# Attention and two feed-forward blocks on one core: the rows of maxima are written into q's stack by DMAs of GpSimd's queue in place of SyncE's

## The chip, the cores and the metric

The kernel runs on one core of a Trainium2 chip. The metric is the device time of one execution, in microseconds (us); less is better. Of several runs the median counts. The engines are named as in the profile: PE is TensorE (PEld its weight loads), DVE is VectorE, ACT is ScalarE, POOL is GpSimd, SP is SyncE. SPq marks SP's DMA-issuing instructions.

## The reference

```python
def _attn_ref(q, k, v, g_q, g_k):              # q, k, v: 4 x 12 x 448 x 64
    q_n, k_n = (rmsnorm(q, g_q), rmsnorm(k, g_k))
    scores = 1.0 / np.sqrt(64) * np.matmul(q_n, k_n.transpose(0, 1, 3, 2))
    scores = scores - np.max(scores, axis=-1, keepdims=True)
    attn = np.exp(scores)
    attn = attn / (np.sum(attn, axis=-1, keepdims=True) + 1e-09)
    return np.matmul(attn, v)

def _moe_ref(x, w_in, w_out, g_ln):            # x: 1792 x 768, d_ff 1024
    h = x @ w_in
    solu = h * softmax(h)
    return layer_norm(solu, g_ln) @ w_out

def _moe2_ref(x, w_in, w_out):                 # d_ff 2048
    h = x @ w_in
    return (h - np.tanh(h)) @ w_out
```

The attention output is put into rows of 768 and goes through the first feed-forward block, then the second. Everything is float32.

## The kernel before, in words

float32 products are made of rounded parts: an operand is split into a high part (`hi`) and a rest (`lo`), and `hi*hi + hi*lo + lo*hi` is summed in PSUM.

**Attention.** The 48 heads are taken in 24 pairs `p`, the heads of a pair being `n = 2p` and `n = 2p + 1`. For a pair, q and k are loaded (`load_qk`), normalised (`norm`, whose last products are L266 on POOL), transposed on PE and split (`qk_trans`, giving `wq` and `wk`). Their parts are stacked by DMA into one of three wide buffers each, `Q[p % 3]` (q_157, q_158, q_159 in listings of the built program) and `K[p % 3]` (k_154 to k_156): 128 rows, of which 64 hold one part and 64 another, so that one matmul sums two products.

The softmax needs the maximum of each row of scores. `maxima` makes the high-part scores on PE (`mps`, L350 and L342), and DVE takes their negated maximum (`nm`, L351). `spread` then turns four columns of `nm` into four rows by a transpose on PE (`nmps`, L358), ACT copies these to SBUF (`nt`, L360; 4 partitions x 128), and a DMA of 2 KB lays them as one row of 512 into q's stack (L363). In the stack of k the matching row is ones, so that the second matmul of each score tile adds the negated maximum to the scores. The scores proper are `weights` (`sps`, L386; L380 to L383 for the first pair): for every block of 128 keys two matmuls, of which the first needs the high stack only and **the second needs the row of maxima**. ACT takes the exponential (`pf`, L395), and `pv` multiplies it with v (`pvps`, L409). So for each of the 48 heads there is this line: DVE's maxima, PE's transpose, ACT's copy, the DMA of L363, PE's second `sps` matmul.

**The order.** The parts of attention stand in a list `attn` with a slot and a step each (`at`, `step`): the maxima of head n at steps 4n to 4n+3, `spread` at 4n+4, its weights from 4n+7 (`LAG`). The first feed-forward block (`moe_h`, `moe_x2`, `moe_lnT`, `layer_norm`) is laid over the attention of the next batch by `overlap`, which interleaves the two by costs. Over this a scheduler of the framework orders the instructions of each engine by a simulated timeline, so the final order differs from that of the code.

**The queues.** SP issues nearly all DMAs, in its order: the loads of q, k and v, the stacks (L309, L313, L315, L316), the weights as raw 64-bit words (L115), their converted copies written out and read again (L164, L178, L182), x and x2 (L440, L504, L624), and the 48 rows of L363. An instruction that waits holds up those behind it on the same engine. POOL issues no DMA; in the attention part it does L266, the last subtraction of a weight conversion (L161), the fill of v's ones (L230, a memset), the power in `layer_norm` (L591) and a few copies of zeros (L320).

After the attention (from about 515 us on) the rest of the first block and the second block (`h2`, `out2`) run, with PE busy all the time.

Of the kernel before, what the change touches and what calls it, by code (L numbers as in the profile page):

```python
# [8 lines left out]
F32 = mybir.dt.float32  # L9
# [9 lines left out]
def kernel(  # L19
# [14 lines left out]
    nc = tc.nc  # L34
    B, H, S, D = q.shape
# [19 lines left out]
    NQ = 3  # L55
# [146 lines left out]
    Q, K, qd = [], [], []  # L202
# [6 lines left out]
    QW, GAP = 4 * S + 64, 64  # L209
# [143 lines left out]
    def spread(n):  # L353

        p, i = divmod(n, 2)
        o = 64 * i if p == 0 else 64 - 64 * i
        ps = ps_m.tile([128, 128], F32, tag="m", name="nmps")
        nc.tensor.transpose(ps[:4], nm_t[p][:, 3 * i:3 * i + 4], idf)  # L358
        nt = A["small"].tile([4, 128], F32R, tag="nt", name="nt")
        nc.scalar.activation(out=nt, in_=ps[:4], func=AF.Copy)  # L360

        c = ((2 + i) * S + GAP if p == 0 else QO[i, 1]) - GAP * i
        nc.sync.dma_start(out=Q[p % NQ][o:o + 1, c:c + S + GAP].bitcast(F32), in_=nt.bitcast(F32))  # L363

    def weights(n, j):

# [85 lines left out]
    for p in range(NP):  # L452
        s = 2 * p
        at(s - 7, 0, load_qk, p)
        if 1 <= p <= NQ:
            at(s - 2 if p < NQ else 4, 1, fill, p % NQ)
            at(s - 2 if p < NQ else 4, 1, fill_q, p % NQ)
        at(s, 1, load_v, p)
        at(s - 3, 1, norm, p)
        at(s - 2, 2, qk_trans, p, 1)  # L460
        at(s - 1, 0, qk_trans, p, 0)
        for i in range(2):
            n, z = s + i, 4 * (s + i)
            for j, c in enumerate((3, 0, 1, 2) if i == 0 else (4, 5, 6)):
                step(z + j, maxima, p, c)
            step(z + 4, spread, n)
            for j in range(3):
                step(z + LAG + j, weights, n, j)
                step(z + LAG + 4 + j, pv, n, j)
        step(z + LAG + 3, weights, s + 1, 3)  # L470
        step(z + LAG + 4, pv_tails, s)
        step(z + LAG + 4, pv_fin, s)
        step(z + LAG + 6, pv_fin, s + 1)
        step(z + LAG + 8, x_norm, p)
# [237 lines left out]
    for z in range(2):  # L712
        o = slice(64 * z, 64 * z + 64)
# [165 lines left out]
```

## Time and the profile before

| | before |
|---|---|
| runs | 1109.31 us median of 3 (1105.35 to 1111.76) |
| profiled execution: span from the first to the last instruction | 1107.5 us |
| profiled execution: its own time | not recorded apart from the span |
| PE busy / PEld busy | 1043.3 us (94%) / 864.2 us (78%) |
| DVE / ACT / POOL busy | 690.5 / 493.1 / 236.4 us |
| mean granted TensorE clock | 0.983 |
| q's rows of maxima (L363) | 48 DMAs of 2 KB, all of SP |

Busy time of an engine is the time in which its instructions run; the issue of a DMA is not counted in it. In rows of waits, a row says who waited (engine, line, tile), for what, the total in us, the number of times and the longest one. "x2" behind an instruction in a timeline is a run of two, told as one; a bracket behind it is the idle time of the engine just before and what ended it.

### The profile page before, as it was taken

To read this page: it belongs to the slowest core of one execution; us is meant where nothing else is said; L and a number is where in the kernel's file an instruction comes from. 1 tells how busy PE (TensorE), PEld (TensorE's weight loads), DVE (VectorE), ACT (ScalarE), POOL (GpSimd) and SP (SyncE) were. 2 spreads that over 40 slices of the span, in tenths; PEclk is the share of its full clock that TensorE was granted. 3 is DMA by queue.
4 is the path that set the end of the run, shared out by engine and by line. 5 is a ranking of instruction groups with operands and counts; after the bars stand their busy time and mean duration, and the time that the engine had idled before them with its cause. 6 is when DMAs were issued, how large, how long until landed. Compare 5 with 4: busy or idle time off the path is not lost.

```text
span 1107.5 us, 15169 instructions
## 1 busy us (share of the span) xinstructions
PE 1043.3 (94%) x5348; PEld 864.2 (78%) x5348; DVE 690.5 (62%) x1311; ACT 493.1 (45%) x994; POOL 236.4 (21%) x204
## 2 busy tenths in 40 slices
PE   4989999989887899999999999999999999999998
PEld 2555566648664678778889989898999989898988
DVE  8766686787787453633684066475767666675444
ACT  4667776777677455555255154311212121212110
POOL 2511123121102110001420034242414141322000
PEclk9999999989988999999999999999999999999999
DMA  7987789866996987666786443021112111110004
GB/s 182 274 227 192 179 216 281 207 181 178 284 320 185 327 229 216 192 209 203 227 291 208 138 162 95 23 74 39 57 40 59 55 58 58 57 57 1 1 29 171
DMA packets 113743, 171.16 MB, mean 155 GB/s; under 512 B 31940, under 2 KB 79492, under 8 KB 113668
## 3 DMA queue, kind: packets, MB, share of 16 engines
q1 hardware_dynamic: 112368, 170.20, 52.8%
q8 instruction: 42, 0.69, 0.3%
q14 instruction: 33, 0.27, 0.1%
q10 hardware_dynamic: 1300, 0.01, 0.1%
HBM read 109.32 MB, written 29.10 MB: 125 GB/s over the span
## 4 chain that ended last, share of the span: by engine, by line
PE 72%; DMA 15%; DVE 6%; ACT 4%; issue 1%; SPq 1%; POOL 1%; ACTq 0%; DVEq 0%; POOLq 0%
PE pvps L409 9%; PE ops L191 7%; PE ops L192 7%; PE ops L190 7%; PE h2ps L191 7%; PE h2ps L192 7%; PE h2ps L190 7%; PE sps L386 4%; DMA raw<-in_moe_w_out_dram 3%; PE x2ps L190 3%; PE x2ps L191 3%; PE x2ps L192 3%; DMA q<-nt 2%; DMA raw<-in_moe_w_in_dram 2%; DMA w<-w_in 2%; PE mps L350 1%
## 5 line engine op out<-in xcount | busy, mean ns | idle before, releaser
L820 DVE TENSOR_TENSOR ob<-ops,ob 128x384 f32<-128x384 f32 x196 | 108.5, 554 | 104.1 <-PE ops L192 103.6
L161 POOL TENSOR_TENSOR w<-val,w 128x512 fp32r<-128x512 f32 x60 | 82.5, 1377 | 424.6 <-ACT w L160 397.0
L409 PE MATMUL pvps<-pf,va 128*128 128x448 f32 (+1 forms) x384 | 164.9, 598 | 0.9 <-ACT pf L395 0.9
L191 PE MATMUL ops<-w,gT 128*128 128x384 f32 x448 | 150.6, 336 | 0.0
L190 PE MATMUL ops<-w,gT 128*128 128x384 f32 x448 | 150.3, 336 | 0.0
L192 PE MATMUL ops<-w,gT 128*128 128x384 f32 x448 | 150.2, 335 | 0.0
L351 DVE TENSOR_REDUCE nm<-mps 128x1 f32<-128x448 f32 x168 | 102.6, 617 | 71.1 <-PE mps L350 61.2
L192 PE MATMUL h2ps<-x2s,w 128*128 128x512 f32 (+1 forms) x384 | 140.9, 367 | 0.0
L386 PE MATMUL sps<-q,k 128*128 128x448 f32 (+1 forms) x368 | 118.1, 415 | 24.2 <-DMA q<-nt 9.7
L191 PE MATMUL h2ps<-x2s,w 128*128 128x512 f32 (+1 forms) x384 | 140.9, 367 | 0.0
L190 PE MATMUL h2ps<-x2s,w 128*128 128x512 f32 (+1 forms) x384 | 140.5, 366 | 0.0
L797 ACT ACTIVATE th<-h2ps 128x512 f32<-128x512 f32 (+1 forms) x64 | 34.8, 544 | 182.5 <-PE h2ps L192 182.3
L386 PEld LDWEIGHTS sps<-q,k 128*128 128x128 f32 (+1 forms) x368 | 63.0, 186 | 60.2 <-ACT pf L395 17.6
L395 ACT ACTIVATE pf<-sps 128x448 f32<-128x448 f32 x167 | 88.3, 539 | 38.5 <-PE sps L386 32.5
L409 PEld LDWEIGHTS pvps<-pf,va 128*128 128x128 f32 (+1 forms) x384 | 63.4, 202 | 42.9 <-issue 35.6
L190 PE MATMUL hps<-w,xs 128*128 128x256 f32 (+1 forms) x276 | 90.6, 329 | 2.6 <-DMA w<-w_in 2.6
L266 POOL TENSOR_TENSOR qn<-qk,rr 112x512 f32<-112x512 f32 x44 | 49.0, 1135 | 195.8 <-DVE rr L247 74.7
L350 PE MATMUL mps<-k,q 128*128 128x448 f32 (+1 forms) x144 | 78.4, 553 | 11.1 <-ACT pf L395 3.3
L191 PEld LDWEIGHTS ops<-w,gT 128*128 128x128 f32 x448 | 84.2, 188 | 4.7
L190 PEld LDWEIGHTS ops<-w,gT 128*128 128x128 f32 x448 | 84.2, 188 | 4.4
L192 PE MATMUL hps<-w,xs 128*128 128x256 f32 (+1 forms) x276 | 85.9, 313 | 0.0
L191 PE MATMUL hps<-w,xs 128*128 128x256 f32 (+1 forms) x276 | 85.7, 311 | 0.0
(118 smaller groups left out, 2042.0 us busy)
## 6 DMA issues: line engine op xcount, KB each, us to landing
w<-w_out SPq DMA_DIRECT2D x48, 512.0 KB
raw<-in_moe_w_in_dram SPq DMA_DIRECT2D x36, 512.0 KB
raw<-in_moe_w_out_dram SPq DMA_DIRECT2D x36, 512.0 KB
w<-w_in SPq DMA_DIRECT2D x24, 512.0 KB
k<-wk SPq DMA_DIRECT2D x46, 224.0 KB
q<-wq SPq DMA_DIRECT2D x46, 224.0 KB
w_in<-w SPq DMA_DIRECT2D x12, 512.0 KB
w_out<-w SPq DMA_DIRECT2D x12, 512.0 KB
```

The lines of the kernel that those rows point to most:

```text
L161: nc.gpsimd.tensor_tensor(out=w[:, 1], in0=x, in1=w[:, 0].bitcast(F32), op=ALU.subtract)
L190: nc.tensor.matmul(ps, lhsT=a[0], rhs=w[0], start=first, stop=False)
L191: nc.tensor.matmul(ps, lhsT=a[0], rhs=w[1], start=False, stop=False)
L192: nc.tensor.matmul(ps, lhsT=a[1], rhs=w[0], start=False, stop=last)
L266: eng.tensor_tensor(out=qn[:, a].rearrange("p c h d -> p h c d"), in0=t[:, a], in1=rr[:, a].rearrange("p h (c o) -> p h c o", o=1).to_broa ...
L350: nc.tensor.matmul(ps, lhsT=qh[:, f:f + 128], rhs=kh, start=True, stop=True)
L351: nc.vector.tensor_reduce(out=nm_t[p][:, c:c + 1], in_=ps, axis=AX.X, op=ALU.max, negate=True)
L386: nc.tensor.matmul(o, lhsT=K[p % NQ][:, i, z, k0:k0 + m], rhs=qcols(Q[p % NQ], slice(0, 128), p, i, z), start=(z == 0), stop=(z == 1))
L395: nc.scalar.activation(out=x, in_=ps, func=AF.Exp)
L409: nc.tensor.matmul(pv_t[n], lhsT=w, rhs=pc_t.pop((n, j))[r], start=first, stop=last)
L797: nc.scalar.activation(out=th, in_=ps, func=AF.Tanh)
L820: nc.vector.tensor_tensor(out=o, in0=ps, in1=o, op=ALU.add)
```

## The change

One line of `spread`: the DMA is issued on GpSimd's queue instead of SyncE's.

```diff
@@ def spread(n)
         nt = A["small"].tile([4, 128], F32R, tag="nt", name="nt")
         nc.scalar.activation(out=nt, in_=ps[:4], func=AF.Copy)
 
         c = ((2 + i) * S + GAP if p == 0 else QO[i, 1]) - GAP * i
-        nc.sync.dma_start(out=Q[p % NQ][o:o + 1, c:c + S + GAP].bitcast(F32), in_=nt.bitcast(F32))
+        nc.gpsimd.dma_start(out=Q[p % NQ][o:o + 1, c:c + S + GAP].bitcast(F32), in_=nt.bitcast(F32))
```

The order of the built program changes with it, on the queues and, through the scheduler, on other engines.

SP, in the middle of the attention (pair 12; q and k are the stacks, xd the attention's output, va the tile of v), as a difference:

```order
 L236 DMA va<-in_v_dram 128x1x64
 L440 DMA xd<-xo 128x448
-L363 DMA q_157<-nt 1x4x128
 L309 DMA q_158<-wq 64x2x448 x2
 L313 DMA q_158<-wq 64x448 x2
-L363 DMA q_157<-nt 1x4x128
 L316 DMA k_156<-wk 64x448 x2
```

The two rows of the pair leave SP; the stacks of the next pair follow the store of x directly.

POOL, from pair 7 to pair 9 (qn is the normalised q and k, w a converted weight tile), as a difference:

```order
+L363 DMA q_158<-nt 1x4x128
+L363 DMA q_159<-nt 1x4x128
 L161 TENSOR_TENSOR w_1450<-val,w_1450 128x512
 L161 TENSOR_TENSOR w_1726<-val,w_1726 128x512
+L363 DMA q_159<-nt 1x4x128
 L266 TENSOR_TENSOR qn<-qk,rr 112x2x4x64 x2
 L161 TENSOR_TENSOR w_1739<-val,w_1739 128x512
 L230 MEMSET va 128x7x64
+L363 DMA q_157<-nt 1x4x128 x2
 L161 TENSOR_TENSOR w_1752<-val,w_1752 128x512
```

The rows now stand between POOL's own instructions, and those behind them wait for ACT's copy with them.

PE, around the first use of pair 2's rows (the stack q_159), as a difference:

```order
-L386 MATMUL sps<-q_159,k_156 128x448 x2
+L386 MATMUL sps<-q_159,k_156 128x448
+L409 MATMUL pvps<-pf,va 128x448 x3
 L342 MATMUL mps<-wk,qd_151 128x448
 L358 MATMUL nmps<-idf,nm 4x128
+L386 MATMUL sps<-q_159,k_156 128x448
+L409 MATMUL pvps<-pf,va 128x448 x2
 L276 MATMUL qkps<-idf,qn 128x112 x4
-L409 MATMUL pvps<-pf,va 128x448 x3
-L386 MATMUL sps<-q_159,k_156 128x448 x2
-L409 MATMUL pvps<-pf,va 128x448 x3
+L386 MATMUL sps<-q_159,k_156 128x448 x2
```

The second `sps` matmul, the one that needs the row, now has three `pvps` matmuls, the `mps` and the next transpose ahead of it.

## Rows read from the trace of the kernel before

**Rows 1.** The page's chain that ended last, by line, shares of the span.
```profile
PE pvps L409 9%; PE ops L191 7%; PE ops L192 7%; PE ops L190 7%; PE h2ps L191 7%; PE h2ps L192 7%; PE h2ps L190 7%; PE sps L386 4%; DMA raw<-in_moe_w_out_dram 3%; PE x2ps L190 3%; PE x2ps L191 3%; PE x2ps L192 3%; DMA q<-nt 2%; DMA raw<-in_moe_w_in_dram 2%; DMA w<-w_in 2%; PE mps L350 1%
```

**Rows 2.** Windows: length, busy us per engine, PE clock, DMA share, GB/s.
```profile
0.00:500.00 500.00, 441.54 (x2113) 314.76 (x2113) 340.17 (x704) 327.75 (x707) 92.65 (x105) 0.96 0.82 227
500.00:1107.00 607.00, 601.73 (x3237) 549.39 (x3235) 350.34 (x607) 165.31 (x288) 143.73 (x99) 1.00 0.30 95
```

**Rows 3.** Waits of PE from 0 to 510 us.
```profile
PE sps L386 <- DMA q<-nt: 9.7, 7, 2.7
PE sps L386 <- ACT pf L395: 9.0, 11, 1.9
PE sps L386 <- DVE nm L351: 4.7, 4, 2.9
...
PE hps L190 <- DMA w<-w_in: 2.6, 4, 0.9
...
PE sps L383 <- DMA q<-nt: 0.6, 1, 0.6
```

**Rows 4.** Timeline around four of PE's eight stops for a row.
```profile
22.32 0.27 ACT L360 ACTIVATE nt<-nmps 4x128 fp32r<-4x128 f32 x1 [0.41 <-PE nmps L358]
25.07 0.71 PE L383 MATMUL sps<-q,k 64*128 64x448 f32 x1 [0.62 <-DMA q<-nt]
...
55.48 0.27 ACT L360 ACTIVATE nt<-nmps 4x128 fp32r<-4x128 f32 x1 [0.52 <-PE nmps L358]
55.77 0.76 SPq L363 DMA_DIRECT2D q<-nt  x1
62.40 0.47 PE L386 MATMUL sps<-q,k 128*128 128x448 f32 x1 [2.73 <-DMA q<-nt]
...
217.34 0.25 ACT L360 ACTIVATE nt<-nmps 4x128 fp32r<-4x128 f32 x1
219.59 0.66 SPq L363 DMA_DIRECT2D q<-nt  x1
222.61 0.47 PE L386 MATMUL sps<-q,k 128*128 128x448 f32 x1 [1.57 <-DMA q<-nt]
...
239.09 0.25 ACT L360 ACTIVATE nt<-nmps 4x128 fp32r<-4x128 f32 x1
244.15 0.74 PE L386 MATMUL sps<-q,k 128*128 128x448 f32 x1 [1.73 <-DMA q<-nt]
```

**Rows 5.** Timeline: copies and the weight loads that need their rows, calm pairs.
```profile
73.18 0.27 ACT L360 ACTIVATE nt<-nmps 4x128 fp32r<-4x128 f32 x1 [0.52 <-DMA qk<-in_k_dram]
75.94 0.30 PEld L386 LDWEIGHTS sps<-q,k 128*128 128x128 f32 x2 [0.41 <-DVE nm L351]
...
126.51 0.27 ACT L360 ACTIVATE nt<-nmps 4x128 fp32r<-4x128 f32 x1 [0.52 <-PE nmps L358]
129.51 1.10 PEld L386 LDWEIGHTS sps<-q,k 128*128 128x128 f32 x6 [0.36 <-DVE nm L351]
...
353.18 0.25 ACT L360 ACTIVATE nt<-nmps 4x128 fp32r<-4x128 f32 x1
355.04 0.57 PEld L386 LDWEIGHTS sps<-q,k 128*128 128x128 f32 x2 [0.55 <-ACT pf L395]
```

**Rows 6.** Windows of a stop and of two half-clock stretches, columns as before.
```profile
59.40:62.40 3.00, 0.27 (x3) 0.01 (x1) 1.11 (x1) 0.21 (x1) 0.00 (x0) 1.00 0.99 270
...
63.26:66.66 3.40, 3.40 (x11) 1.43 (x8) 2.50 (x6) 2.43 (x7) 0.00 (x0) 0.50 0.61 149
...
387.53:390.93 3.40, 3.40 (x9) 2.05 (x7) 1.25 (x2) 0.54 (x1) 0.00 (x0) 0.50 0.96 308
```

**Rows 7.** SP's own waits, from 0 to 500 us, the first row of L363.
```profile
SPq L363 <- ACT pf L395: 15.5, 8, 3.3
```

**Rows 8.** POOL's lines: min, median, max ns of L161; group of L591.
```profile
L161 POOL TENSOR_TENSOR w<-val,w x60: 1265/1293/2642, 24.3 to 1024.6; 128x512 fp32r<-128x512 f32 x60
...
L591 POOL TENSOR_TENSOR rs<-rs,mhalf 128x1 f32<-128x1 f32 x14 | 9.3, 671 | 76.7 <-DVE rs L590 64.9 <-DVE rs L593 10.1 <-DVE rr L247 1.7
```

## The prediction

> **What bounds the kernel now.** I read the chain of waits first, by line [rows 1]. The reader is to see that PE's lines fill most of it, and that `DMA q<-nt`, the row of maxima on its way into q's stack, holds 2% of the span, some 22 us: small, but the largest entry after PE's lines and the weight loads. The windows say where time can be won at all [rows 2]: from 500 us on PE is busy 601.7 of 607 us, so nothing there is to be had; before it PE stands still 500 - 441.5 = 58.5 us, and a microsecond taken out of that moves all that follows. PE's waits split that idle time [rows 3]: the row of maxima is behind 9.7 us of it at `sps`, and 0.6 us at the first pair, 10.3 us in eight stops. ACT's exponentials (9.0) and DVE's maxima (4.7) come next at the same line.
>
> The timeline shows such a stop whole [rows 4]. ACT's copy ends at 55.75, SP issues at once, and PE, which could have gone on at 62.40 - 2.73 = 59.67, goes at 62.40. So the row took 6.65 us where 3.9 were to be had. I call the first number its delay (end of the copy to PE going) and the second its **room**. The issue is 0.7 us of it, so nearly 6 us are flight, and in that window the DMA engines are busy 0.99 of the time [rows 6]: the 2 KB lie behind megabytes which SP issued before. At 217 us the other part shows: the copy ends at 217.59, SP issues 2.0 us later, because it stands at something before it.
>
> A stop costs twice. After that of 2.73 us the granted clock is 0.50 from 63.26 to 66.66, that is 1.2 instead of 2.4 GHz, with PE busy throughout [rows 6]: 3.4 us at half speed do 1.7 us of work. Five such stretches, the first and the last of which are shown, begin within 3 us of a stop for a row.
>
> **The change, part by part.** *SP loses 48 issues.* Each is about 0.66 us [rows 4], 32 us of SP's time, and with them its waits for ACT at L363, of which the largest row alone is 15.5 us [rows 7]. The stacks and loads behind them go out earlier. I cost that at nothing: PE's waits for a weight load are 2.6 us [rows 3], which bounds the gain, and the DMA engines are at their limit where loads are late. Cover: the loads are issued ahead; were it gone, this 2.6 us would grow first.
>
> *POOL gains 48 issues.* No row shows a DMA of POOL. Its price lies between that of POOL's smallest work of the kind, 0.67 us for one column (L591), and that of a subtraction over 512 columns, 1.3 us (L161) [rows 8]. I take 1.0, near the first, since a DMA of four pieces is little work. For the flight I take what SP's rows need in calm stretches: a copy that ended at 73.45 had landed before the second load of the pair that starts at 75.94, so at most 2.6 us after the copy, of which 0.66 are issue; and in the pair at 353 us at most 2.0 us, of which 1.3 are flight [rows 5]. So copy to landing is 1.0 + 1.3 to 1.0 + 1.9, or 2.3 to 2.9 us; I take **3.0** for all, with a little for crowded stretches. The ends: 2.0 us, if POOL issues as fast as SP, and 6.65, the delay of [rows 4], if the flight stays as long as it is.
>
> The Trainium skill (DMA: Bandwidth & Descriptors, Latency and other measured facts) gives the first byte about 1 us after a DMA of GpSimd and 0.6 after one of SyncE; no run here shows that yet, and an estimate from it would be SP's 2.6 plus 0.4, 3.0 us as well.
>
> *The eight stops.* A delay of 3.0 us ends each stop whose room is 3.0 or more. The rooms in [rows 4], as above: 1.86 at the first pair (22.59 to 25.07 - 0.62), 3.92, 3.45 and 3.08; the other four have more. So seven stops go, 9.7 us, and the first grows from 0.62 to 1.14.
>
> *The calm rows pay.* There the row comes just in time now. Rooms in [rows 5], up to the load that needs the row, each load taking 0.19: 2.6 us at 73, 3.6 at 127 (the last of the six loads), 2.0 at 353. Of the first heads of the five pairs copied between 73 and 127 these are the first and the last, the three others about 3. New stops at 3.0: 0.4 and 1.0 us. Second heads have more room, since a whole head's scores come before theirs.
>
> Idle time: 10.3 goes, 1.1 + 0.4 + 1.0 = 2.5 comes, net -7.8. Clock: five stretches of 1.7 go, 8.5; that the two new stops of about 1 us draw one each is the dear assumption, and I take it: 3.4 comes back, net -5.1. Together -12.9.
>
> *What is late next.* At the lines where PE stopped, ACT's and DVE's work is the other thing it waits for [rows 3], 13.7 us beside 9.7. Where the row comes earlier, some of those stops stay with another name. I count two thirds: **-8.6**.
>
> *POOL's queue.* In the order of before and after, most pairs have both rows together, ahead of L266. In five pairs POOL's own work stands between, which holds the second row only, by a subtraction of 1.3 us or two; second heads have the room. What is queued behind a waiting row is L266, L161 and L591; L266's products go to PE's transposes of a later pair, L161's to a store for later. I cost that at nothing; uncovered, it is 1.3 us for each such pair.
>
> *The schedule.* It moves little. Three `pvps` matmuls more before pair 2's row add room at the longest stop.
>
> The sum against the profiled execution: 1107.5 - 8.6 = 1098.9 of span. The median of the runs is 1.8 above the span of before, so 1100.7; I say **1101**.
>
> **The rivals.** *The flight stays long* (chance 0.10). If POOL's row waits in the same DMA engines behind the same bulk, only SP's queueing is saved: 2.0 us at 217, and at the longest stop nothing. That takes away about half of the stops, -5 + 2.5 of idle, and two of five stretches, -3.4, so about -6, two thirds of it -4: 1105. For it: the DMA share of 0.99. Against: 2 KB need not lie behind another queue's megabytes. The Trainium skill (DMA: Bandwidth & Descriptors, Issuing engines are not separate DMA queues) says that all issuers run on the same 16 engines and that another issuer saves only issue time; by that rule this case would hold.
>
> *The next wait takes over* (0.12). ACT's and DVE's lines stop PE at the same places; with a quarter of the sum left, 1106.
>
> *POOL is slow, and it gets slower* (0.15). It is decided at a delay of about 4.1 us from the copy. At 4.0 the stops are 2.1, 0.1, 0.6 and 0.9 in [rows 4], 1.4, three of 1.0, 0.4 and 2.0 in [rows 5]: 10.5, as much as goes. At 5.0 each of the ten is one more, 20.5 against 10.3, and there are ten stretches of half clock against five: +10.2 + 8.5 = 18.7, two thirds 12.5, so 1122. For it: a subtraction of POOL was stretched from 1.27 to 2.64 us, so something can hold POOL. Against: its median is 1.29 [rows 8], so that is rare. The Trainium skill (SBUF — State Buffer, SBUF: two separate sides) says that a DMA of GpSimd cannot write its descriptors while DVE runs an operation that takes the shared port; by that rule POOL's issue would be long where DVE converts weights, and this case would hold there.
>
> *More than that* (0.08): the whole 12.9 and loads earlier by 2.6 us, 1094.
>
> **How the numbers follow.** The forecast has 0.55, with a range of its own from 1094 to 1106. Half a per cent, about what a measurement of this kernel can tell from no change, is 5.5 us: faster is below 1103.8, slower above 1114.9. The forecast gives 0.46 to faster and 0.09 to the same; the long flight 0.02 and 0.08; the next wait 0.10 to the same and 0.02 to slower; slow POOL 0.13 to slower and 0.02 to the same; the last 0.08 to faster. That is 0.56, 0.29, 0.15. For 8 in 10 the range goes from 1090 to 1114: it takes in the whole sum with a few us for the schedule, no gain, and a delay a little above 4.1.
>
> **What would show it.** Right: POOL's DMA instructions take about 1 us; PE's wait for `DMA q<-nt` falls from 10.3 to some 3 us, and is at the first pair and at calm pairs; the half-clock stretches behind PE's stops for a row are gone; SP has no L363. Wrong: POOL's issue of 2 us or more, or waits of `sps` for the row at every calm pair; or the waits for the row gone and PE idle as long before 500 us, with ACT or DVE named. The prediction fails also if the new order delays L266 or `layer_norm` behind a row that waits.

## The result and the profile after

The changed kernel is slower: 1118.88 us median (1116.77 to 1121.97, 6 runs) against 1107.37 us (1104.63 to 1111.76, 6 runs) of before, a ratio of 1.0104 with a 95% interval from 1.0074 to 1.0134, or 11.5 us. The forecast was 1101 us with a range that ended at 1114. Its profiled execution took 1116.77 us, with a span of 1114.5. In the experiments below one run of e1_first_sp (1124.58 us) and one of s1_sp_order (1131.38 us) were in a slower state; they count in the medians and not in the ratios.

The rows of maxima in the changed kernel, by tile (minimum, median, maximum in ns; then from the start of the issue to the landing in us):

```profile
L363 POOL DMA_DIRECT2D q<-nt x48: 521/556/772, 22.6 to 497.8; - x48
...
DMA to landing us min/median/max: 1.5/3.2/8.5
```

GpSimd issues a row in 0.556 us, less than the 1.0 that I assumed. But it lands after 1.5 us only at best, after 3.2 in the median and 8.5 at worst. The stretch makes a difference: here are the landings from 220 to 265 us, where the DMA engines are busy 0.64 of the time, and from 265 to 330 us, where they are busy 0.97.

```profile
DMA to landing us min/median/max: 1.6/2.6/3.6
...
DMA to landing us min/median/max: 4.8/5.3/8.5
```

The windows that answer to [rows 2]:

```profile
0.00:500.00 500.00, 436.96 (x2083) 312.04 (x2084) 342.05 (x704) 322.80 (x698) 117.72 (x153) 0.96 0.81 225
500.00:1107.00 607.00, 605.25 (x3245) 550.61 (x3244) 348.46 (x603) 169.86 (x296) 144.12 (x99) 1.00 0.29 94
```

Before 500 us TensorE stands still for 500 - 436.96 = 63.0 us, where it was 58.5. That is 4.5 us more. All of the loss is ahead of 500 us, for the last copy of `nt` is 7.60 us later and the whole span 7.0. The mean granted clock there is 0.96 in both, but the two decimals hide a few us: the stretches at 0.50 ahead of 500 us sum to 44.4 us where they were 37.5. At half speed that is (44.4 - 37.5) / 2 = 3.5 us, an estimate, and with the 4.5 us about the whole loss. It comes early; the first 70 us before and after (the clock is the third figure from the end):

```profile
0.00:70.00 70.00, 48.74 (x153) 27.37 (x154) 52.10 (x121) 40.47 (x87) 23.91 (x31) 0.95 0.90 231
...
0.00:70.00 70.00, 47.56 (x128) 26.74 (x128) 52.41 (x112) 35.38 (x77) 23.74 (x34) 0.85 0.78 211
```

TensorE's waits up to 510 us, which answer to [rows 3]:

```profile
PE sps L386 <- ACT pf L395: 8.6, 12, 2.2
PE hps L190 <- DMA w<-w_in: 5.4, 2, 4.2
PE x2ps L190 <- DMA w<-w_out: 4.8, 1, 4.8
PE pvps L409 <- ACT pf L395: 4.7, 6, 2.6
PE sps L383 <- DMA q<-nt: 4.6, 1, 4.6
...
PE sps L386 <- DVE nm L351: 2.8, 6, 0.9
...
PE sps L386 <- DMA q<-nt: 1.7, 4, 0.7
```

The wait that the change was to remove did shrink, from 9.7 to 1.7 us. Four others grew: the first pair's row from 0.6 to 4.6, the weights of the first block's input projection (`hps`) from 2.6 to 5.4, and those of its output projection (`x2ps`), one wait of 4.8 where the same view of before has

```profile
PE x2ps L190 <- DMA w<-w_out: 1.3, 2, 1.0
...
PE pvps L409 <- ACT pf L395: 0.9, 3, 0.4
```

The last of these lines is the fourth: `pvps` waits 4.7 us for ACT's exponentials where it was 0.9.

To see where the time goes I compare when ACT makes the same copy of `nt` in two traces. The shift (after less before) is +11.36 us at the 5th copy (66.83 against 55.48; the shifts are of unrounded times), +6.05 at the 12th, +0.40 at the 27th (239.49 against 239.09), +1.04 at the 31st, +5.39 at the 32nd, +9.08 at the 37th and +7.60 at the last. So there are three stretches: a loss up to 67 us, a gain up to 239 us, and a second loss from 282 us on.

The first loss begins at the first pair. Timeline of the changed kernel (answers to the first stop of [rows 4]):

```profile
21.67 0.27 ACT L360 ACTIVATE nt<-nmps 4x128 fp32r<-4x128 f32 x1 [0.27 <-PE nmps L358]
...
22.57 0.77 POOL L363 DMA_DIRECT2D q<-nt  x1 [15.86 <-ACT nt L360]
...
28.38 0.71 PE L383 MATMUL sps<-q,k 64*128 64x448 f32 x1 [4.58 <-DMA q<-nt]
```

The copy is earlier than before, and TensorE goes 3.3 us later. That stop I had put at 1.14 us. From 35.30 to 38.70 us TensorE is busy only 1.93 us; then the granted clock (the figure ahead of the DMA share) falls from 2.4 to 1.2 GHz and stays there for 20 us:

```profile
38.71:59.19 20.48, 20.45 (x46) 11.33 (x46) 13.78 (x27) 8.33 (x19) 8.34 (x9) 0.50 0.82 240
```

The second loss begins at 292 us:

```profile
292.02 0.58 PE L190 MATMUL hps<-w,xs 128*128 128x256 f32 x1 [4.23 <-DMA w<-w_in]
```

### The profile page after: what moved, and what is told of

Its sections match the earlier page's. It is cut to its first block, busy times and chain, and to the rows that moved or that the text cites. A ratio compares the mean times of both kernels' runs of the same rounds, so it can differ in the third digit from the quotient of the medians.

```text
span 1114.5 us, 15196 instructions
## 1 busy us (share of the span) xinstructions
PE 1046.2 (94%) x5348; PEld 866.4 (78%) x5348; DVE 693.2 (62%) x1311; ACT 492.7 (44%) x994; POOL 261.8 (23%) x252
## 4 chain that ended last, share of the span: by engine, by line
PE 70%; DMA 13%; DVE 8%; ACT 3%; issue 3%; POOL 1%; SPq 1%; DVEq 0%; POOLq 0%; ACTq 0%
PE pvps L409 8%; PE ops L191 7%; PE ops L192 7%; PE ops L190 7%; PE h2ps L191 7%; PE h2ps L192 7%; PE h2ps L190 7%; PE sps L386 4%; PE x2ps L190 3%; PE x2ps L191 3%; PE x2ps L192 3%; DMA xr<-xd 2%; DMA w<-w_in 2%; DVE nm L351 2%; DMA q<-nt 2%
## 5 line engine op out<-in xcount | busy, mean ns | idle before, releaser
L161 POOL TENSOR_TENSOR w<-val,w 128x512 fp32r<-128x512 f32 x60 | 81.4, 1360 | 371.4 <-ACT w L160 363.8
L386 PE MATMUL sps<-q,k 128*128 128x448 f32 (+1 forms) x368 | 118.9, 414 | 13.7 <-ACT pf L395 8.6
L386 PEld LDWEIGHTS sps<-q,k 128*128 128x128 f32 (+1 forms) x368 | 62.7, 185 | 49.4 <-ACT pf L395 16.3
L190 PE MATMUL hps<-w,xs 128*128 128x256 f32 (+1 forms) x276 | 91.1, 331 | 5.5 <-DMA w<-w_in 5.4
L363 POOL DMA_DIRECT2D q<-nt x48 | 26.7, 556 | 259.4 <-ACT nt L360 202.4
L190 PE MATMUL x2ps<-lnT,w 128*128 128x384 f32 (+1 forms) x240 | 80.5, 335 | 6.0 <-DMA w<-w_out 5.7
L192 PE MATMUL hps<-w,xs 128*128 128x256 f32 (+1 forms) x276 | 85.9, 314 | 0.0
L138 POOL TENSOR_SCALAR val<-raw 128x512 f32<-128x512 f32 x48 | 79.7, 1660 | 25.6 <-DMA raw<-in_moe_w_out_dram 10.8
```

What stands on the lines that cost most here:

```text
L138: nc.gpsimd.tensor_scalar(out=fv, in0=fh, scalar1=2.0 ** -15, scalar2=None, op0=ALU.max)
L161: nc.gpsimd.tensor_tensor(out=w[:, 1], in0=x, in1=w[:, 0].bitcast(F32), op=ALU.subtract)
L190: nc.tensor.matmul(ps, lhsT=a[0], rhs=w[0], start=first, stop=False)
L192: nc.tensor.matmul(ps, lhsT=a[1], rhs=w[0], start=False, stop=last)
L363: nc.gpsimd.dma_start(out=Q[p % NQ][o:o + 1, c:c + S + GAP].bitcast(F32), in_=nt.bitcast(F32))
L386: nc.tensor.matmul(o, lhsT=K[p % NQ][:, i, z, k0:k0 + m], rhs=qcols(Q[p % NQ], slice(0, 128), p, i, z), start=(z == 0), stop=(z == 1))
```

## The experiments

Executions of one kernel differ: beside the first four experiments the kernel before ran 31 times, from 1099.07 to 1113.06 us. So sizes below are ratios to runs of before taken beside the kernel, with 95% intervals (they are not quite the quotients of the medians), and single traces are used for the place of a loss and for waits that return in several of them. The median of before was 1106.20, 1108.06, 1106.94, 1109.01 and 1106.71 us in the five groups of experiments; 0.1% is 1.1 us.

| kernel | rows of maxima issued by | order of the rest | median us | ratio |
|---|---|---|---|---|
| changed kernel | POOL | its own ("new") | 1118.88 | 1.0104 (1.0074 to 1.0134) |
| e8_after_again | POOL | new | 1121.05 | 1.0134 (1.0079 to 1.0188) |
| e1_first_sp | SP for pair 0, POOL | its own | 1110.84 | 1.0036 (1.0010 to 1.0062) |
| e2_late_sp | POOL up to pair 12, then SP | its own | 1112.17 | 1.0055 (1.0023 to 1.0087) |
| e3_mid_pool | POOL for pairs 1 to 12, else SP | its own | 1106.19 | 0.9996 (0.9966 to 1.0026) |
| e4_act_queue | ACT | its own | 1111.07 | 1.0048 (1.0013 to 1.0083) |
| e5_warm | POOL, one DMA earlier | new | 1117.28 | 1.0101 (1.0059 to 1.0143) |
| e7_sp_twin | POOL, twins on SP | its own | 1116.73 | 1.0080 (1.0053 to 1.0108) |
| e9_pool_twin | SP, twins on POOL | its own | 1114.14 | 1.0055 (1.0021 to 1.0089) |
| e6_only_first | POOL for pair 0, else SP | its own | 1112.65 | 1.0040 (1.0018 to 1.0063) |
| r1_order_before | POOL | that of before ("old") | 1112.81 | 1.0043 (1.0018 to 1.0068) |
| r2_order_after | SP | new | 1119.47 | 1.0111 (1.0075 to 1.0147) |
| r3_first_sp | SP for pair 0, POOL | old | 1108.14 | 1.0013 (0.9985 to 1.0041) |
| s1_sp_order | SP | new on SP, old elsewhere | 1118.07 | 1.0081 (1.0042 to 1.0121) |
| s2_engine_order | SP | old on SP, new elsewhere | 1148.26 | 1.0349 (1.0314 to 1.0384) |
| s3_act_pinned | ACT | old | 1113.55 | 1.0053 (1.0025 to 1.0082) |
| s4_warm_pinned | POOL, one DMA earlier | old | 1111.31 | 1.0028 (1.0004 to 1.0051) |
| t1_order_late | SP | new from pair 13 on | 1116.03 | 1.0096 (1.0068 to 1.0124) |
| t2_order_early | SP | new up to pair 12 | 1110.42 | 1.0026 (1.0002 to 1.0050) |

### Which pairs lose it

```diff
-        nc.gpsimd.dma_start(out=Q[p % NQ][o:o + 1, ...
+        (nc.sync if p == 0 else nc.gpsimd).dma_start(...        # e1_first_sp
+        (nc.sync if p > 12 else nc.gpsimd).dma_start(...        # e2_late_sp
+        (nc.gpsimd if 0 < p < 13 else nc.sync).dma_start(...    # e3_mid_pool
+        nc.scalar.dma_start(...                                 # e4_act_queue
```

e1_first_sp, expected:

> The first pair's two rows go back to SyncE's queue, the other 46 stay on GpSimd's. Theory START (the first row lands 3.3 us later on GpSimd's queue, SyncE's bulk goes out beside it, and TensorE's rise to full clock and its next rows slip with it: 11.4 us lost by 67 us of the span): the shift at the fifth stop (the copy of nt at 55.48 us before, 66.83 us after) falls to within 2 us of before, and the time to about 1108 us (1105 to 1111). Theory LATE (the loss is made from 285 to 420 us, by the weights' loads in SyncE's new order): the shift of 6.5 us there stays, and the time falls by less than 6 us. Theory ORDER (any other order of SyncE's queue scatters the time, no single row is the cause): 1113 to 1121 us with the early shift still over 5 us.

e2_late_sp, expected:

> The rows of pairs 13 to 23 go back to SyncE's queue; those of pairs 0 to 12 stay on GpSimd's. Theory LATE: the shift made from 285 to 420 us (6.5 us) goes, the wait for the output projection's weights falls from 4.8 us towards 1.3, and the time is about 1112 us (1110 to 1115). Theory START alone: the 11.4 us at 67 us stay and are given back by 265 us as in the changed kernel; what happens later does not depend on the queue, so 1117 to 1121 us. Theory ORDER: no more than 3 us either way.

e3_mid_pool, expected:

> Only the rows of pairs 1 to 12 go by GpSimd's queue; pair 0 and pairs 13 to 23 stay on SyncE's. START and LATE together: neither loss is made and the gain of 10.2 us between 67 and 265 us stays, at least in part (the stops that it removes in that stretch): 1096 to 1103 us, faster than before. If the gain between 67 and 265 us was only the recovery of the time lost at the start (the loads run ahead while TensorE is late, so that later waits are shorter), it is not there without the loss: 1105 to 1110 us. ORDER: 1110 to 1120 us.

e4_act_queue, expected:

> All 48 rows go by ScalarE's queue, behind the copy that makes them, so SyncE is relieved as with GpSimd's queue, but GpSimd's way of issuing is left out. If the loss is that of GpSimd's queue (a first packet 2.9 us after the issue at the first row, landings of 1.5, 3.2 and 8.5 us), the first row lands within 0.5 us of its time before and the time is below 1112 us, unless ScalarE's own issue time (unknown; at 0.5 to 1 us each for 48 of them 24 to 48 us of ScalarE's time, part of it on the chain) takes it back. If the loss is that SyncE's bulk is no longer held behind the rows (START by crowding, or ORDER), it stays: 1115 to 1125 us, with the first row late as in the changed kernel.

With the first pair back on SyncE a loss of 0.36% is left, with the late pairs back one of 0.55%, and with both back none: each half seems to cost about as much as the other. But pairs 1 to 12 by GpSimd's queue also gained nothing (0.9996), though it is in their stretch that the changed kernel gained 10 us of shift. So those 10 us were no gain of the change but a recovery of a TensorE that was late at the start. e6_only_first, further down, has it too, with the rows of pairs 1 to 12 on SyncE: its shift is +10.04 us at the 5th copy and +1.92 at the 27th. The rows on ScalarE's queue lose as well (1.0048) with the first row on time (TensorE goes at 24.58 us). So GpSimd's queue need not be the cause, though ScalarE's own 48 issues may be part of that loss.

### What the queue does, and what is only late once

e5_warm puts one DMA of 2 KB on GpSimd's queue at 6.65 us; nothing waits for it.

```diff
     make_identity(nc, idf)
+    warm = const.tile([1, 512], F32, name="warm")
+    nc.gpsimd.dma_start(out=warm, in_=idf[:4, :])
```

> The changed kernel with one more DMA of 2 KB on GpSimd's queue at the very start, which nothing waits for. Theory FIRST USE (the queue's first DMA is slow because it is the first: issue 0.77 us against a median of 0.556, first packet 2.9 us later): the first row is then an ordinary one and lands some 1.5 us after its issue as the calm rows do, TensorE's wait of 4.58 us at the first pair falls below 1.5, and the time falls from about 1117.5 us to 1108 to 1114. Theory CROWD (the row goes out while SyncE's load of 512 KB and the q stacks fill the engines): the wait stays over 4 us and the time is within 3 us of the changed kernel's, 1115 to 1121 us.

```profile
23.32 0.53 POOL L363 DMA_DIRECT2D q<-nt  x1 [15.90 <-ACT nt L360]
...
26.35 0.71 PE L383 MATMUL sps<-q,k 64*128 64x448 f32 x1 [1.74 <-DMA q<-nt]
```

The same row, no longer the first on its queue, is issued in 0.53 us where it was 0.77, and TensorE waits 1.74 us where it was 4.58. The first use of the queue costs 2.8 us there (4.58 - 1.74); s4_warm_pinned below repeats it with the order held. Yet the kernel is not measurably faster (1.0101; its shift is +0.7 us at the 12th copy, but +9.5 at the last). The time that the first pair loses is not what the changed kernel loses at its end.

The twins keep the old queue busy, or only the new one:

```diff
+        sc = A["small"].tile([4, 128], F32, tag="sc", name="sc")
+        nc.sync.dma_start(out=sc, in_=nt.bitcast(F32))          # e7_sp_twin; e9_pool_twin: gpsimd here, sync below
         nc.gpsimd.dma_start(out=Q[p % NQ][o:o + 1, ...
```

> The rows stay on GpSimd's queue, and in the place of each row SyncE's queue issues a twin that copies the same four lines of maxima into a scratch tile that nothing reads, so SyncE waits and issues as before. Theory RELEASE (the loss comes from SyncE being free: without its 48 waits its bulk transfers start earlier, in another order, and meet the rows and the weights): both losses go, the first row lands within 1 us of before, and the time is at most 1109 us. Theory POOL PATH (GpSimd's queue itself delivers late, or its issue holds up GpSimd's other work): the early shift of 7 to 11 us and the late one stay, and the time is 1115 to 1122 us.

> The mirror of the twin: the rows stay on SyncE's queue as before the change, and GpSimd issues a twin of each into a scratch tile that nothing reads. Theory POOL PATH by GpSimd's time (48 issues of 0.56 us, each waiting in GpSimd's order for its copy of nt, hold up the splits and constants behind them): the late loss of about 5 us comes without the rows having moved, 1110 to 1114 us. Theory RELEASE, or POOL PATH by slow delivery: nothing waits for the twins, 1104 to 1109 us, the same as before.

e7_sp_twin refutes RELEASE as I had put it: SyncE waits and issues 48 times as before, the first row on GpSimd's queue is as late (TensorE's wait is 4.34 us), and the loss is there. e9_pool_twin came out, at 1114.14 us, where the theory by GpSimd's time had put it (1110 to 1114), though nothing waits for its twins. Its trace does not show that theory: of 1106.45 us, it is the shortest of its ten runs and has no late loss. And r3_first_sp below, with 46 issues on GpSimd and the order held, costs 1.4 us (-1.7 to +4.5). So the cause stays open here. The kernel has an order of its own, as each kernel so far had, and that is the flaw of all these experiments.

e8_after_again, the changed kernel once more:

> The changed kernel once more, unaltered, for its time beside these runs and for a second trace. Every theory: 1115 to 1121 us, 1.0% over before. Where the losses are made: if the three steps of the first trace (11.4 us lost by 67 us, 10.2 gained by 265, 6.5 lost by 420) belong to the kernel and not to one execution, the second trace shows them with at most 3 us of difference each.

Its second trace has the same stretches: +9.49 us at the 5th copy, -1.58 at the 27th, +6.47 at the 32nd, +7.18 at the last. They belong to the kernel. So does the place: `hps` waits for `w_in` (2.50 us at 293.10) and `x2ps` for `w_out` (4.01 at 373.82).

### The queue and the order taken apart

The scheduler reorders all engines when the queue is changed. To change one without the other, a table at the end of the program gives each engine's instructions, by the number that the code gave them, in the order in which another built program has them, and ties each behind the one ahead of it, for the issue alone (no wait comes with it). No run times the kernel before with a table of its own order. But in the traces the 5348 matmuls stand in r3_first_sp in the order of before, and in r2_order_after in that of the changed kernel, with no difference by line and tile, while between these two orders some 350 differ; and r3_first_sp, with a table, is not measurably slower than before. The rows of maxima are not in the tables where they change queues; the scheduler places them.

```diff
+_ORDER = {
+    "Pool": ...
+def _replay(nc, tc):
+    by = {i.name: i for i in nc.cur_bb.bb.instructions}
+    info = mybir.DependencyInfo(mybir.DependencyClass.NoSync, mybir.DependencyReason.DATA)
+    for e, text in _ORDER.items():
+        names = [f"I-{int(x, 36)}" for x in text.split()]
+        names = [n for n in names if n in by]
+        for a, b in zip(names, names[1:]):
+            tc.add_manual_dep(by[b], a, info, reason="replay")
...
         tile_attention_solu_tanh_kernel(tc, *args)
+        _replay(nc, tc)
```

> All 48 rows on GpSimd's queue, but every other instruction stands in the order of before on its engine (a table pins it; the rows are put between GpSimd's own instructions by the scheduler). Theory ORDER (the loss from 285 to 420 us is made by the new order that the scheduler gave the engines, not by the queue): no late loss, x2ps waits for the output weights about 1 us instead of 4 to 5, and 1104 to 1110 us; the late first row may leave 1 to 3 us of that. Theory DELIVERY (GpSimd's queue lands the rows late wherever SyncE's bulk is in the engines, and that costs the time): the loss stays, 1115 to 1122 us.

> The mirror: the 48 rows on SyncE's queue as before the change, and every other instruction in the order of the changed kernel. Theory ORDER: the late loss comes with the order, 1113 to 1120 us, with waits of 4 to 5 us for the weights of both projections near 292 and 373 us. Theory DELIVERY: the queue of before brings back the time of before, 1104 to 1110 us.

> As r1_order_before, with the two rows of the first pair on SyncE's queue. If ORDER holds, what is left is the gain that was forecast for the 46 other rows without the late first row: between 1094 us (the whole predicted sum) and 1107 us (nothing), and I expect 1101 to 1107 since pairs 1 to 12 alone gave nothing. If DELIVERY holds: 1110 to 1117 us, as the first run of this study.

> Only the first pair's two rows go by GpSimd's queue, all others by SyncE's, in the order that the scheduler makes of that. The first row lands 3 us late as in the changed kernel and 5 to 10 us are lost by 60 us of the span. Theory START (that loss reaches the end): 1112 to 1118 us. Theory ABSORBED (the stretch from 190 to 245 us, where the shift of the changed kernel fell from 6 to 0 us in two traces, takes it back whatever the queue): 1105 to 1110 us.

This is a table of two by two. Old order: SyncE 1, GpSimd 1.0043. New order: SyncE 1.0111, GpSimd 1.0104 and 1.0134. **The order alone, with not one row moved to GpSimd, loses all that the change loses**, and in it the queue no longer matters. In the old order GpSimd's queue costs 4.8 us (2.0 to 7.5), and with the first pair on SyncE (r3_first_sp) 1.4 (-1.7 to +4.5), which cannot be told from nothing. e6_only_first, the first pair alone on GpSimd's queue, costs 0.40%, which agrees; but it has an order of its own again.

In r3_first_sp, where 46 rows are on GpSimd's queue and the order is held, TensorE's waits up to 510 us are

```profile
PE sps L386 <- ACT pf L395: 8.5, 11, 2.0
PE sps L386 <- DVE nm L351: 5.5, 6, 3.0
PE sps L386 <- DMA q<-nt: 4.9, 5, 2.3
PE pvps L409 <- ACT pf L395: 4.1, 4, 3.2
...
PE sps L383 <- DMA q<-nt: 2.5, 1, 2.5
```

and in its windows

```profile
0.00:500.00 500.00, 440.37 (x2109) 314.92 (x2110) 345.38 (x704) 327.68 (x704) 116.72 (x151) 0.96 0.82 226
```

The waits for rows at `sps` L386 are about half of before (9.7 to 4.9 us), that of the first pair, on SyncE as before, is 2.5 us where it was 0.6, and TensorE is busy no longer than in [rows 2] (440.37 against 441.54). `pvps` now waits 4.1 us for ACT's exponentials where it was 0.9, and the wait for the maxima is 5.5 where it was 4.7. A single trace does not put the shorter waits down to the queue: t2_order_early below, with all rows on SyncE, has 4.8 us at L386 too. The wait of `pvps` is firmer: in the four kernels with the old order and the rows off SyncE it is 4.1 (r3), 3.3 (r1), 3.5 (s4) and 3.6 us (s3), and 0.9 both before and in t2.

### Which part of the order

> Rows on SyncE's queue; SyncE's other DMAs in the order of the changed kernel, TensorE, VectorE, ScalarE and GpSimd in the order of before. Theory LOADS (the weights are late because SyncE's new order loads them late): 1114 to 1121 us, with the waits of 4 us for both projections' weights. Theory ENGINES (TensorE's new order asks for the weights before they can be there): 1104 to 1110 us.

> The mirror: rows on SyncE's queue, all of SyncE's DMAs in the order of before, the four other engines in the order of the changed kernel. LOADS: 1104 to 1110 us. ENGINES: 1114 to 1121 us. If both of these kernels lie between (1109 to 1114), each order costs a part, and neither theory is right alone.

> All 48 rows on ScalarE's queue, every other instruction in the order of before. If leaving SyncE's queue is worth something once the order is held, this shows it without GpSimd's late first row: 1098 to 1105 us. If the stops for the rows are only handed on to the next wait (as 46 rows on GpSimd's queue gave 1.0013), 1105 to 1111 us: ScalarE's 48 issues of 0.58 us may cost some of that.

> As r1_order_before (all rows on GpSimd's queue, old order, 1112.8 us), with one DMA of 2 KB more on GpSimd's queue at the start, which nothing waits for. Theory FIRST USE: the wait at the first pair falls from 4.0 us to below 2 and the time to that of r3_first_sp, 1106 to 1110 us. If the first pair's loss is that of the rows meeting SyncE's bulk, 1111 to 1115 us.

SyncE's new order alone costs 0.81%. Its trace has the wait of `x2ps` again (3.8 us), but more of it is new waits for the rows, 16.9 us in eight, so it is no clean copy of the loss. The mirror is far worse than both (1.0349), outside what either theory said: the two orders fit each other, and to mix them makes other waits. Whether SyncE's or the engines' order is to blame is not to be had in this way. s3_act_pinned says once more that leaving SyncE's queue gains nothing when the order is held. In its trace the rows' waits do go, from 10.3 to 1.7 us, and the three others at `sps` and `pvps` rise from 14.6 (9.0, 4.7 and 0.9) to 25.2:

```profile
PE sps L386 <- ACT pf L395: 11.7, 14, 2.9
...
PE sps L386 <- DVE nm L351: 9.9, 10, 3.0
...
PE pvps L409 <- ACT pf L395: 3.6, 4, 2.7
...
PE sps L386 <- DMA q<-nt: 1.7, 3, 0.9
```

ScalarE's own 48 issues, of 0.58 us in the median, may be part of that. s4_warm_pinned lies between r1 and r3; its first wait is 1.66 us where r1 has 4.01, but the difference in time of r1 and s4 is inside their intervals. Their traces, one each, show what can go with a late first row: r1 has a stretch at 0.50 of 17.06 us from 38.31 us, s4 one of 3.41 us from 50.31 us, and by the 5th copy r1 is 8.42 us late and s4 0.57. At the last copy 2.72 and 0.51 us are left.

The last two runs split the program instead. Their tables are the orders that the scheduler gave to e2_late_sp (new up to pair 12, then old) and to a kernel with the rows of pairs 13 to 23 alone on GpSimd's queue (old, then new), so they hold together; all rows are on SyncE's queue.

> Rows on SyncE's queue. The order is that of before up to pair 12 and that of the changed kernel from pair 13 on, on every engine. If the loss of r2_order_after (12 us, of which 6 were made between 265 and 420 us in its trace) is made late: 1113 to 1120 us, with the wait of about 4 us for the input projection's weights near 290 us. If it is made early: 1105 to 1110 us.

> The mirror: the order of the changed kernel up to pair 12, that of before from pair 13 on, rows on SyncE's queue. If the loss is made late: 1106 to 1111 us, the early 5 us at 55 us of the span being given back by 90 us as in r2_order_after. If early: 1112 to 1118 us.

The new order from pair 13 on costs 10.6 us (7.5 to 13.7), that up to pair 12 costs 2.9 (0.2 to 5.5). Shifts of ACT's copies against the trace of before, in us:

| copy of nt (before, us) | changed | again | r2 | t1 | t2 | r1 |
|---|---|---|---|---|---|---|
| 5th (55.48) | +11.36 | +9.49 | +5.13 | +0.63 | +6.76 | +8.42 |
| 27th (239.09) | +0.40 | -1.58 | +0.05 | +0.47 | +0.32 | +2.28 |
| 31st (281.70) | +1.04 | +3.72 | +2.21 | +2.10 | +0.31 | +3.54 |
| 32nd (289.28) | +5.39 | +6.47 | +6.13 | +6.61 | +0.40 | +3.35 |
| 37th (372.17) | +9.08 | +10.72 | +10.38 | +10.96 | +0.90 | +1.69 |
| last (489.62) | +7.60 | +7.18 | +8.53 | +10.08 | -0.44 | +2.72 |

Wherever the new order stands late (changed, again, r2, t1), 2.7 to 4.5 us come between the 31st and the 32nd copy and 3.7 to 4.4 more by the 37th; where the old one stands (t2, r1, and r3 with +0.01, -0.59 and -0.14), they don't, whatever the queue. The place in t1_order_late, SyncE's issues and the stop:

```profile
284.48 0.36 SPq L182 DMA_DIRECT2D w<-w_in  x1
284.89 0.76 SPq L440 DMA_DIRECT2D xd<-xo  x1
287.43 0.67 SPq L363 DMA_DIRECT2D q<-nt  x1
288.20 0.64 SPq L309 DMA_DIRECT2D q<-wq  x1
288.93 0.54 SPq L182 DMA_DIRECT2D w<-w_in  x1
...
293.25 0.58 PE L190 MATMUL hps<-w,xs 128*128 128x256 f32 x1 [4.40 <-DMA w<-w_in]
```

and in the kernel before:

```profile
282.65 0.54 SPq L440 DMA_DIRECT2D xd<-xo  x1
283.28 0.93 SPq L363 DMA_DIRECT2D q<-nt  x1
284.32 0.86 SPq L182 DMA_DIRECT2D w<-w_in  x2
285.27 0.64 SPq L309 DMA_DIRECT2D q<-wq  x1
...
290.03 0.39 PE L190 MATMUL hps<-w,xs 128*128 128x256 f32 x1 [0.87 <-DMA w<-w_in]
```

Before, the two loads of `w_in` follow each other; in the new order the store of x, a row and a stack stand between them. But that is not what costs the time. The view of each load (who waited for it) gives the 4.40 us of t1 to the first of the two, issued at 284.48, and nothing to the second, of 288.93; before, too, the 0.87 us belong to the first, of 284.32. So the load is issued at the same time in both, TensorE asks at about the same moment (290.03 - 0.87 = 289.16 and 293.25 - 4.40 = 288.85), and gets it 3.2 us later. From the issue to TensorE going it takes 5.71 us before (5.19 in t2, 6.31 in r3, and r1 does not wait for it), and with the new order 9.06, 7.90, 8.01, 8.77 and 7.79 us (changed, again, r2, t1, e5). Why it takes longer is not shown. Behind the stop TensorE runs at 1.2 GHz for a while: the granted clock is 0.50 from 293.0 to 296.4 us in t1.

The stop of `x2ps` near 373 us comes back in all four too (4.80, 4.01, 4.32, 3.80). There the new order does load late. In the changed kernel the store of x (L440) stands ahead of the loads of `w_out`:

```profile
360.72 0.34 SPq L440 DMA_DIRECT2D xd<-xo  x1
...
365.22 1.95 SPq L182 DMA_DIRECT2D w<-w_out  x4
...
371.38 0.69 PE L190 MATMUL x2ps<-lnT,w 128*128 128x384 f32 x1 [4.80 <-DMA w<-w_out]
```

and before it stands behind the first three, and TensorE does not wait:

```profile
359.11 1.67 SPq L182 DMA_DIRECT2D w<-w_out  x3
360.88 0.65 SPq L440 DMA_DIRECT2D xd<-xo  x1
...
364.45 0.69 PE L190 MATMUL x2ps<-lnT,w 128*128 128x384 f32 x1
```

The first load goes out 6.1 us later (365.22 against 359.11), and TensorE's first `x2ps` of this stretch comes 6.9 us later. That the place in SyncE's order alone does it is not shown: the stop is there in s1_sp_order (3.8 us), but in s2_engine_order (4.4 us) as well.

## Why the prediction was wrong

**The step that failed** is "*The schedule.* It moves little." I had shown three places of the new order and read none of the places that hold the weights' loads. The order is worth 12.3 us (8.3 to 16.3) by r2_order_after, as much as the whole change; t1_order_late puts 10.6 us of it behind pair 12, where two waits for weights return; and none of my rivals was that the order by itself costs time. The sentence on SyncE's relief had the right object, for I wrote that the waits for a weight load, 2.6 us, "would grow first"; I costed it at nothing because the loads are issued ahead. In the new order that of `w_out` is issued 6.1 us later, behind a store, and that of `w_in`, issued no later, takes 2 to 3.4 us longer to reach TensorE.

**The sum for the rows** failed too, without the order, and by its last step. Moved with the order held (r3_first_sp), 46 rows leave TensorE standing still as long as before (59.6 us up to 500 us against 58.5). This is the rival "the next wait takes over", to which I gave 0.12: I counted two thirds of 12.9 us, a gain of 8.6, and a loss of 1.4 (-1.7 to +4.5) was measured. s3_act_pinned says the same of ScalarE's queue, and shows the waits handed on. In the changed kernel one of my signs of being wrong came in the main: the waits for the row at L386 are nearly gone (1.7 us), TensorE is idle no less (63.0 us), and ACT is named for more (`pvps`, 4.7 us). The Trainium skill (DMA: Bandwidth & Descriptors, Issuing engines are not separate DMA queues) says that another issuer saves issue time alone; r3_first_sp and s3_act_pinned, at 1.0013 and 1.0053, show no gain beyond that.

**The delay.** The issue was put at 1.0 us and is 0.556; copy to landing was put at 2.3 to 2.9 us, while from issue to landing alone the median is 3.2 and the largest 8.5. I had taken the flight from SyncE's calm rows; in crowded stretches it stays long (5.3 us in the median from 265 to 330 us), which was the first rival's mechanism. So of seven stops some go and some shrink. The rival with a slow POOL had put its time, 1122 us, nearest to what was measured, but that is luck: its reason was a long issue, and the longest of the 48 is 0.772 us.

**The first pair** was to grow from 0.62 to 1.14 us. It is 4.58, 4.19, 4.01 and 4.11 us in the traces of the changed kernel, its repetition, r1 and e6, and 1.74 and 1.66 where the queue had been used before (e5, s4). I had no row for the first use of a queue, and should have given the first stop a bound of its own. With the old order GpSimd's queue costs 4.8 us, of which r3 without the first pair keeps 1.4; with the new order it adds nothing that could be measured.

**The clock** was to give back 5.1 us. It gave nothing back: the stretches at 1.2 GHz ahead of 500 us sum to 37.5 us before, 44.4 in the changed kernel and 41.0 in r3. A long one (17.1 to 20.5 us) stands near 38 us in all six traces in which the first pair's row is the first DMA of GpSimd's queue (changed, again, e2, e6, e7, r1), and the early ones of the two with the queue used before last 6.8 and 3.4 us (e5, s4). But it is not the first row's alone, since r2_order_after, with that row on time, has one of 13.66 us from 36.04 us.

**What stays open:** what part of the order (SyncE's or the engines') makes the late loss, beyond the two stops that are shown; why the load of `w_in` takes longer to land in it; and why e9_pool_twin is slower than before. No version was found that beats the kernel before; e3_mid_pool and r3_first_sp cannot be told from it.

## What to carry to other kernels

Where a scheduler orders the instructions, a change of queue is two changes. Pin the order of before and make the change in it, and pin the new order without the change: the two runs say at once which of them the time belongs to. Read the new order at the places where a transfer is waited for with little to spare, not only around the edited line: a load that now stands behind a store is a loss to look for. And ask the trace which load a stop waits for: here, of two that were adjacent and are no longer, it was the one that had not moved. And a wait that a trace names can be removed without gain when the next one stands right behind it; its length is no estimate of what can be had.

## What the runs showed of the hardware

The first DMA on GpSimd's queue took 0.77 us to issue against 0.53 for the same row with one DMA ahead of it, and TensorE waited 2.35 to 2.84 us longer for the row (4.01 against 1.66 in r1 and s4, 4.58 against 1.74 in the changed kernel and e5). It took 0.77 us wherever it stood: at 6.65 us of the span in e5, at 41.08 in r3. From issue to landing a DMA of 2 KB on this queue took 1.5 us at the least, 3.2 in the median and 8.5 at the most; the median was 2.6 us where the DMA engines were busy 0.64 of the time and 5.3 where they were busy 0.97. And a loss can be given back: the shift was +6.13, +4.27 and +8.29 us at the 22nd copy (186 us) in the changed kernel, its repetition and r1, and +0.40, -1.58 and +2.28 at the 27th (239 us). In this kernel, how late TensorE is at one place says little about the end.
